# Loads of x gated by earlier batches, zero fills moved behind the softmax, the band copied in four pieces, and a new order, in a convolution and token-mixing kernel

## The chip, the cores and the metric

The kernel runs on one core of a Trainium2 chip. The metric is the device time of one execution in microseconds (us); lower is better. PE is the matrix engine (PEld its weight loads), DVE, ACT and POOL are the vector, scalar and general engines, SP is the engine that here only issues transfers. "A DMA" is a transfer that an engine issues and 16 DMA engines carry out.

## What is computed

```python
# x: (8, 4224, 192), weight: (8 heads, 7 taps)
w = softmax(weight)                       # over the 7 taps
x_pad = zeros of 6 rows in front of x
out[b, s, head, g] = sum_k w[head, k] * x_pad[b, s + k, head, g]     # 24 columns g a head
x = out
wq, wk = x @ w_q, x @ w_k                 # (8, 4224, 64)
W_tok = (1 / 8) * einsum('bsd,btd->bst', wq, wk)
mixed = einsum('bst,btd->bsd', W_tok, x)  # 4224 x 4224 weights a batch, never formed
result = relu(mixed) @ w_out              # (8, 4224, 192) float32
```

Since nothing nonlinear stands between the products, `mixed = wq @ (w_k.T @ (x.T @ x)) / 8`: a 192 x 192 Gram matrix a batch takes the place of the token weights.

## The kernel before, in words

**Stages of a batch.** A batch of 4224 rows is cut into 35 chunks of 122 rows. A chunk of x is loaded with the 6 rows before it, 128 rows in all, and turned from float32 to bfloat16 by the load itself (`XW`, which holds all eight batches; issued by POOL, L565). The causal convolution is a matmul with a banded 128 x 128 matrix a head (`BAND`): `conv`, L651, four operations of two heads each for a group of chunks (groups of 9 chunks in batch 0, of 18 and 17 in the others, L315). ACT or DVE copies the result to `Y` (L671). PE then transposes Y (`tr_lo` L691, `tr_hi` L726; copies by DVE, L698 and L733), forms wq from the transposes (`wq`, L751 and L755, five operations a batch, j = 0 to 4), and adds up the Gram matrix from Y itself (L787). A small product chain (L808 to L861) makes the 192-wide mixing matrix of the batch. Then, for each of five token blocks, `mix_lo` (L878) and `mix_hi` (L890) apply it to wq, ACT and DVE take the relu (L907, L908), `fin_hi` (L935) and `fin_lo` (L955) multiply by w_out, ACT or DVE copies to one of four output slots (L970), and SP stores the slot (L978). `mix_lo` and `fin_hi` use the array as two halves of 64 rows, all others as two halves of 64 columns. The helper `halves` (L391, L392) issues the two column halves of `conv`, of `fin_lo` and of some smaller products, `turn_halves` (L395, L396) those of the transposes, so that these lines stand for several stages and the tile names tell them apart.

**What sets the order.** Every operation is entered in a planner with its engine or engines, an estimated length in ns, the operations that it needs, and a due time. The due times of the program text (`vt=`) are not used: `add` (L381) takes them one by one from the list `TURNS`. The planner lays the operations one after another on five engine queues by its estimates; among the operations that are ready on an engine, it takes the one with the lowest due time, where PE adds `STAY` to an operation that would change its way of halving the array. The result is a fixed order on each engine. An engine waits (with semaphores) before an instruction for what the instruction needs; `after` only orders the planning. An engine never passes over an instruction that waits.

**Start.** DVE fills small tiles (L409 to L422), among them zeros in the tiles that need them only later (`zero_w`, `zero_yt`, `zero_q`, two `zero_k`, `zero_m`). SP loads `weight` (L402). POOL builds the identity `IDENT` (L426), from which DVE makes `step`, `other`, `own` (L435 to L457). Then the softmax: `mx` (L461, needs `weight`), `sub`, `mine`, ACT's exponentials `ex` (L482), `sm`, `rc`, `wn`, `taps` (L494, needs `own`). PE spreads the taps into two banks with eight matmul pairs (`fill`, L512), and ACT copies the one bank, DVE the other, into `BAND` (L527): two copies of 512 columns. All convolutions need both.

**Loads of x.** `gen_load` (L535) makes for each group one DMA of its whole chunks, and one each for the first chunk of a batch and for the last, short one: 34 in all. In batch 0 a DMA brings 7 to 9 chunks, in the others 17 or 16. They wait for no step of the computation: POOL issues them one behind the other from the start, and the planner takes it that a group lands at 5000 ns plus 260 ns for each chunk so far (`at`, L559). The three weight matrices are loaded by SP once group 1 of batch 0 has landed (L589).

**The loop.** Batch b's conv, transposes, wq, Gram and mixing matrix are entered together with the `mix` blocks of batch b - 1 (L988 to L1007). Y and wq are kept for two batches.

Of the kernel before, what the change touches and what calls it, by code (L numbers as in the profile page):

```python
# [13 lines left out]
    int(t) / 1000  # L14
    for t in """
# [50 lines left out]
""".split()  # L66
]

COL2, ROW2 = "128x64", "64x128"


class Op:


    n = 0

# [27 lines left out]
class Planner:  # L104

    LAT = {"PE": 240.0, "ACT": 145.0, "DVE": 140.0, "POOL": 150.0, "SP": 0.0}
    SWITCH = 145.0

    STAY = 0.865

    HOLD = 1

    def __init__(self, nbank, first_bank):
        self.ops = []
        self.order = []
# [162 lines left out]
def bass_lightweight_conv__then__hypermixer_token_mlp_kernel(  # L280
# [25 lines left out]
    t = 0  # L306
# [173 lines left out]
    def exps(e, op):  # L480
# [19 lines left out]
        220, wn, -7.5,  # L500
    )
    taps.needs.append(own)


    bands = []
    for q0, engine in ((0, "ACT"), (4, "DVE")):
# [552 lines left out]
```

## Time and profile before

| | |
|---|---|
| median of 3 executions | 177.7 us (177.54 to 178.31) |
| the profiled execution | 177.53 us, of it 175.7 us from the first to the last instruction (the span) |
| DVE busy | 118.0 us (67%) |
| ACT busy | 123.5 us (70%) |
| POOL busy | 30.3 us (17%), the last load issued at 52.5 us |
| loads of x | 13.61 MB written as bfloat16 |
| stores | 44 DMAs, 25.95 MB |
| batch 0: first conv, first Gram | 8.8 us, 13.1 us |
| first conv of batches 1 to 7 | 23.5, 34.4, 47.7, 67.9, 90.2, 105.7, 129.7 us |

How to read the profile: times are us from the first instruction. A row of the timeline has the start, the length, the engine, the line, the operation, what it writes and reads, and in brackets how long the engine stood idle before it and what ended that. "issue" as the end of an idle time means that the engine waited for nothing that the profile shows. A row of the windows has, for a stretch of time, the busy us of each engine with the count of its instructions, the granted clock, the DMA share (time of all queues' packets over that of 16 DMA engines, above 1 where packets of two queues overlap) and the GB/s. The DMA queue q0 carries the loads of x, q1 the other loads and the stores, q8 instructions. In the list of loads, "to landing" counts from the issue.

### The profile page before, as it was taken

The numbers are of one execution on the slowest core, as the hardware profiler recorded it, in microseconds if no ns is written. First come the engines' busy times: TensorE is split into PE (matmuls) and PEld (weight loads), VectorE is DVE, ScalarE is ACT, GpSimd is POOL, SyncE is SP. The second block draws the span as 40 slices with busy tenths as digits, with TensorE's granted clock in tenths as the row PEclk, the third lists the DMA queues.
The fourth block names the chain that finished last, engine by engine and source line by source line (L and its number), as shares of the span: only waits on it lengthen the run. The fifth ranks groups of instructions, "written<-read, shape, count | busy, mean of one in ns | idle before, by whom it ended". The sixth has DMA issues, their size and how long they took to land.

```text
span 175.7 us, 7099 instructions
## 1 busy us (share of the span) xinstructions
PE 157.1 (89%) x3226; PEld 121.7 (69%) x3226; DVE 118.0 (67%) x216; ACT 123.5 (70%) x206; POOL 30.3 (17%) x39
## 2 busy tenths in 40 slices
PE   0289799888999999899989979999999999999990
PEld 0179666776787787668778766878767777877550
DVE  6556587765766677586787738689688675765740
ACT  3243677597787948668648747888888896698980
POOL 7999452524230000000000000000000000000000
PEclk9999999999999999999999999999999999999995
DMA  3999999999999999999999999067283045987787
GB/s 30 162 189 186 205 191 193 191 196 277 193 279 194 286 309 268 343 250 243 304 264 282 237 194 348 24 244 297 103 343 127 4 175 216 356 347 309 265 303 262
DMA packets 48157, 40.36 MB, mean 230 GB/s; under 512 B 37632, under 2 KB 40960, under 8 KB 48128
## 3 DMA queue, kind: packets, MB, share of 16 engines
q0 software_dynamic: 36128, 13.61, 65.1%
q1 hardware_dynamic: 12000, 26.31, 40.9%
q8 instruction: 25, 0.41, 0.9%
q14 instruction: 4, 0.03, 0.1%
HBM read 27.56 MB, written 25.95 MB: 305 GB/s over the span
## 4 chain that ended last, share of the span: by engine, by line
PE 88%; issue 4%; DVE 3%; ACT 2%
PE ps L391 25%; PE ps L787 14%; PE ps L935 8%; PE ps L392 7%; PE ps L395 6%; PE ps L726 6%; PE ps L878 5%; PE ps L751 4%; PE ps L890 4%; PE ps L755 4%; PE ps L396 3%; ACT rt L907 1%; ACT out_sb L970 1%; DVE band L527 0%; DVE xw L416 0%
## 5 line engine op out<-in xcount | busy, mean ns | idle before, releaser
L970 ACT COPY out_sb<-ps 128x768 f32<-128x768 f32 (+1 forms) x46 | 34.7, 768 | 15.1 <-PE ps L392 11.3
L671 ACT CAST y<-ps 122x816 bf16<-122x816 f32 (+3 forms) x46 | 35.7, 791 | 13.2 <-PE ps L392 12.8
L907 ACT ACTIVATE rt<-ps 128x1024 bf16<-128x1024 f32 (+3 forms) x44 | 34.1, 800 | 6.4 <-PE ps L878 4.5
L787 PE MATMUL ps<-y 122*64 122x192 bf16 (+4 forms) x840 | 33.8, 222 | 2.2 <-issue 2.2
L970 DVE COPY out_sb<-ps 128x768 f32<-128x768 f32 (+1 forms) x26 | 21.6, 840 | 19.7 <-PE ps L392 18.5
L392 PE MATMUL ps<-wol,rt 128*64 128x192 bf16 x264 | 33.9, 255 | 1.0 <-issue 1.0
L787 PEld LDWEIGHTS ps<-y 122*64 122x64 bf16 (+1 forms) x840 | 31.1, 112 | 4.9 <-issue 2.8
L565 POOL DMA_DIRECT2D xw<-in_x_dram x34 | 29.9, 893 | 22.3 <-issue 21.5
L391 PE MATMUL ps<-wol,rt 128*64 128x192 bf16 x264 | 33.7, 255 | 0.0
L391 PE MATMUL ps<-xw,band 128*64 128x432 bf16 (+3 forms) x144 | 31.8, 335 | 1.5 <-DVE band L527 0.9
L392 PE MATMUL ps<-xw,band 128*64 128x432 bf16 (+3 forms) x144 | 32.1, 337 | 1.1 <-issue 1.1
L391 PEld LDWEIGHTS ps<-wol,rt 128*64 128x64 bf16 x264 | 24.1, 138 | 8.1 <-issue 2.0
L908 DVE TENSOR_SCALAR rt<-ps 128x512 bf16<-128x512 f32 (+3 forms) x36 | 23.6, 674 | 8.2 <-PE ps L878 7.6
L671 DVE CAST y<-ps 122x864 bf16<-122x864 f32 (+3 forms) x26 | 23.6, 912 | 8.0 <-PE ps L392 7.5
L698 DVE COPY ytl<-ps 128x976 bf16<-128x976 bf16 (+1 forms) x40 | 23.0, 591 | 3.9 <-PE ps L396 3.3
L392 PEld LDWEIGHTS ps<-wol,rt 128*64 128x64 bf16 x264 | 24.1, 138 | 1.2 <-issue 1.2
L396 PE MATMUL ps<-ident,y 122*64 122x122 bf16 x280 | 21.1, 219 | 0.0
L395 PE MATMUL ps<-ident,y 122*64 122x122 bf16 x280 | 21.0, 219 | 0.0
L935 PE MATMUL ps<-woh,rt 64*128 64x192 bf16 x264 | 20.4, 250 | 0.2 <-ACT rt L907 0.2
L395 PEld LDWEIGHTS ps<-ident,y 122*64 122x64 bf16 x280 | 18.1, 112 | 2.0 <-issue 0.5
L726 PE MATMUL ps<-ident,y 122*64 122x122 bf16 (+1 forms) x344 | 17.1, 220 | 1.3 <-DVE y L671 0.7
L396 PEld LDWEIGHTS ps<-ident,y 122*64 122x64 bf16 x280 | 17.7, 112 | 0.0
(95 smaller groups left out, 218.8 us busy)
## 6 DMA issues: line engine op xcount, KB each, us to landing
out_dram<-out_sb SPq DMA_DIRECT2D x28, 768.0 KB, 5.1
xw<-in_x_dram POOLq DMA_DIRECT2D x7, 816.0 KB, 33.2
xw<-in_x_dram POOLq DMA_DIRECT2D x7, 768.0 KB, 33.7
out_dram<-out_sb SPq DMA_DIRECT2D x8, 384.0 KB, 3.3
xw<-in_x_dram POOLq DMA_DIRECT2D x2, 432.0 KB, 8.3
out_dram<-out_sb SPq DMA_DIRECT2D x8, 96.0 KB, 4.3
xw<-in_x_dram POOLq DMA_DIRECT2D x1, 384.0 KB, 5.2
xw<-in_x_dram POOLq DMA_DIRECT2D x8, 45.8 KB, 25.0
```

The costliest lines, as they stand in the source:

```text
L391: e.matmul(out[0:64], lhsT[:, 0:64], rhs, **k)
L392: return e.matmul(out[64:128], lhsT[:, 64:128], rhs, **k)
L395: e.transpose(out[0:64], in_[:, 0:64], identity)
L396: return e.transpose(out[64:128], in_[:, 64:128], identity)
L565: lambda e, op, part=part: e.dma_start(*part),
L671: return e.copy(dst, src) if op.engine == "ACT" else e.tensor_copy(dst, src)
L726: last = e.transpose(ps[64 * i : 64 * i + HI, o : o + w], Y[0:w, yb, c, LO:D], IDENT[0:w, 0:w])
L787: mm = e.matmul(bank(GB)[p : p + 64, o : o + z - r], Y[0:w, yb, c, r : r + 64], Y[0:w, yb, c, r:z], start=st, stop=end, skip_group_check=True,
L907: return e.activation(dst, src(), AF.Relu)
L908: return e.tensor_scalar(dst, src(), 0.0, None, op0=ALU.max)
L935: last = e.matmul(bank(op.bank + a)[:, o : o + D], RT[64 * a : 64 * a + HI, slot, 2, i:n:nt], WOH[64 * a : 64 * a + HI, :], start=i == q, ...
L970: return e.copy(dst, src) if op.engine == "ACT" else e.tensor_copy(dst, src)
```

## The change

1. **Loads in four parts, paced.** From batch 1 on, the whole chunks of a group are loaded by two DMAs, the first with half of them rounded up: 9 and 8 chunks, 8 and 8. With the first and the last chunk that is six DMAs a batch and 48 in all. Each now needs a step of an earlier batch (a wait on POOL). For batch 1: the first chunk and first half of group 0 wait for group 2 of batch 0 to have landed, the second half for batch 0's last conv of group 2; group 1's first half waits for batch 0's last conv, the rest for its `wq` j = 0. For batch b from 2 on: first chunk and first half of group 0 wait for `wq` j = 0 of batch b - 2, the second half for j = 1; group 1's first half for j = 2, the rest for j = 3. The loads are entered in the planner beside the conv of their group. The planner now counts 4500 ns from issue to landing from batch 1 on, and fixed landing times in batch 0 (6000, 9900, 12300, 13900 ns).
2. **Zeros behind the softmax.** The six zero fills named above come after `taps` in DVE's order. The due time of `own` goes from -9.28 to -8.19, between `mine` (-8.21) and `sm` (-8.16); before, it stood right behind `other` (-9.29).
3. **Band in four pieces.** Four fills of two matmul pairs each (256 columns), four banks, four copies: ACT, DVE, ACT, DVE.
4. **Order.** All due times of the main part are new, `STAY` goes from 0.865 to 0.954561. The estimates of `ident` (1250 to 700), of the fills (260 to 200) and of the band copies (550 to 340) change with it.

```diff
@@ -11,58 +11,90 @@
 
 
 TURNS = [
-    int(t) / 1000
+    int(t) / 1e6
     for t in """
...
 """.split()
 ]
 
@@ -108,9 +140,9 @@
     LAT = {"PE": 240.0, "ACT": 145.0, "DVE": 140.0, "POOL": 150.0, "SP": 0.0}
     SWITCH = 145.0
 
-    STAY = 0.865
-
-    HOLD = 1
+    STAY = 0.954561
+
+    HOLD = 1.000000
 
     def __init__(self, nbank, first_bank):
         self.ops = []
@@ -426,7 +458,7 @@
         lambda e, op: e.affine_select(
             IDENT[:, :], IDENT[:, :], [[-1, 128]], ALU.is_equal, 0.0, base=0, channel_multiplier=1
         ),
-        1250,
+        700,
         needs=[one],
         vt=-9,
     )
@@ -455,7 +487,7 @@
     own = add(
         "DVE",
         lambda e, op: e.tensor_reduce(OWN[:, :], IDENT[:, :].rearrange("p (k i) -> p i k", i=16), AX.X, ALU.add),
-        200, needs=[ident], vt=-8.92)
+        200, needs=[ident], vt=-7.83)
 
 
     mx = add("DVE", lambda e, op: e.tensor_reduce(WMX[:, :], WT_F[:, :, :], AX.X, ALU.max), 150, needs=[load_w], vt=-8)
@@ -501,38 +533,43 @@
     )
     taps.needs.append(own)
 
+    for zero in (zero_w, zero_yt, zero_q, *zero_k, *(zero_m if isinstance(zero_m, list) else [zero_m])):
+        zero.after.append(taps)
+
 
     bands = []
-    for q0, engine in ((0, "ACT"), (4, "DVE")):
+    for q0, engine in ((0, "ACT"), (2, "DVE"), (4, "ACT"), (6, "DVE")):
 
         def spread(e, op, q0=q0):
             last = None
-            for q in range(q0, q0 + 4):
+            for q in range(q0, q0 + 2):
                 last = halves(
                     e,
                     bank(op.bank)[:, (q - q0) * 128 : (q - q0 + 1) * 128],
                     STEPT[0:112, 112 - 16 * q : 240 - 16 * q],
                     TAPS[0:112, :, :].rearrange("p i h -> p (i h)"),
                     start=q == q0,
-                    stop=q == q0 + 3,
+                    stop=q == q0 + 1,
                     skip_group_check=True,
                 )
             return last
 
-        fill = add("PE", spread, 260, needs=[taps, stept], banks=1, vt=-7 + 0.1 * q0)
+        fill = add("PE", spread, 200, needs=[taps, stept], banks=1, vt=-7 + 0.1 * q0)
 
         def band(e, op, q0=q0, fill=fill):
-            dst = BAND[:, :, 16 * q0 : 16 * q0 + 64]
-            src = bank(fill.bank).rearrange("p (j h) -> p h j", h=H)
+            dst = BAND[:, :, 16 * q0 : 16 * q0 + 32]
+            src = bank(fill.bank)[:, 0 : 32 * H].rearrange("p (j h) -> p h j", h=H)
             return e.copy(dst, src) if op.engine == "ACT" else e.tensor_copy(dst, src)
 
-        bands.append(add(engine, band, 550, drains=fill, vt=-6.9))
+        bands.append(add(engine, band, 340, drains=fill, vt=-6.9))
 
 
     load = {}
-    at = [5000.0]
-
-    def gen_load(b, gi):
+
+    LANDS = [6000.0, 9900.0, 12300.0, 13900.0]
+
+    def gen_load(b, gi, gates=()):
+
         sem = semaphore(f"s_x{b}_{gi}")
         cs = groups_of(b)[gi]
         parts = []
@@ -540,13 +577,17 @@
         full = [c for c in cs if 0 < c < NCC - 1]
         if cs[0] == 0:
             parts.append((XW[KC - 1 : 128, b, 0, :], bass.AP(x_t, base, [[D, CW], [1, D]])))
-        n = len(full)
-        parts.append(
-            (
-                XW[:, b, full[0] : full[0] + n, :],
-                bass.AP(x_t, base + (CW * full[0] - KC + 1) * D, [[D, 128], [CW * D, n], [1, D]]),
+        cut = (len(full) + 1) // 2 if b else len(full)
+        for some in (full[:cut], full[cut:]):
+            if not some:
+                continue
+            parts.append(
+                (
+                    XW[:, b, some[0] : some[0] + len(some), :],
+                    bass.AP(x_t, base + (CW * some[0] - KC + 1) * D, [[D, 128], [CW * D, len(some)], [1, D]]),
+                )
             )
-        )
+        lead = 1 + (cs[0] == 0)
         if cs[-1] == NCC - 1:
             rows = S - (CW * (NCC - 1) - KC + 1)
             parts.append(
@@ -556,7 +597,6 @@
                 )
             )
 
-        at[0] += len(cs) * 260.0
         load[b, gi] = []
         for k, part in enumerate(parts):
             first = (b, gi) == (0, 0) and part[0].shape[1] > 1 and len(part[0].shape) == 3
@@ -564,13 +604,13 @@
                 "POOL",
                 lambda e, op, part=part: e.dma_start(*part),
                 900,
-                needs=[zero_x] if cs[-1] == NCC - 1 else [],
+                needs=[*([zero_x] if cs[-1] == NCC - 1 else []), *(gates[0 if k < lead else 1] if gates else [])],
                 after=[] if first else [ident],
                 dma=(f"x{b}_{gi}", sem, 16),
                 vt=-10 if first else -4 + b + gi * 0.1 + 0.02 * k,
             )
-            op.tail = 1500.0
-            op.lands = at[0]
+            op.tail = 1500.0 if b == 0 else 4500.0
+            op.lands = LANDS[gi] if b == 0 else 0.0
             load[b, gi].append(op)
 
     for gi in range(len(groups_of(0))):
@@ -615,14 +655,11 @@
         cast(WOH[:, :], WHI[:, OS], load_o),
     ]
 
-    for b in range(1, B):
-        for gi in range(len(groups_of(b))):
-            gen_load(b, gi)
-
 
     y_done, y_read = {}, {}
     yt_done, yt_read, yth_read, wq_read, rt_read, m_read = {}, {}, {}, {}, {}, {}
     g_read, gsb_read = None, None
+    conv_op, wq_op = {}, {}
     store_of = {}
     n_rt = n_out = 0
     S_OUT = [semaphore(f"s_o{i}") for i in range(NOUT)]
@@ -670,6 +707,7 @@
                 dst = dst.rearrange("p c (t g) -> p t c g", t=2)
                 return e.copy(dst, src) if op.engine == "ACT" else e.tensor_copy(dst, src)
 
+            conv_op[b, gi] = mm
             ev = add(both, evac, evac_ns(2 * n * GRP), needs=ev_needs, drains=mm, vt=vt, kind="y")
             for c in cs:
                 y_done.setdefault((b, c), []).append(ev)
@@ -759,6 +797,7 @@
 
         mq = add("PE", wq, mm_ns(n, 2), needs=[*{id(r): r for c in cs for r in yt_done[b, c]}.values(), turned, *casts_q],
             after=wfree, banks=1, vt=vt, kind="wq")
+        wq_op[b, j] = mq
         yth_read[b, j] = [mq]
         for c in cs:
             for g in range(0, NCC, 8):
@@ -989,6 +1028,10 @@
         nxt = []
         if b < B:
             for gi in range(len(groups_of(b))):
+                if b == 1:
+                    gen_load(b, gi, ([load[0, 2][-1]], [conv_op[0, 2]]) if gi == 0 else ([conv_op[0, 3]], [wq_op[0, 0]]))
+                elif b:
+                    gen_load(b, gi, ([wq_op[b - 2, 2 * gi]], [wq_op[b - 2, 2 * gi + 1]]))
                 gen_conv(b, gi)
             for c in range(0, NCC, 8):
                 gen_transpose(b, list(range(c, min(c + 8, NCC))))
```

132 rows, old and new, of the table TURNS are left out of this document.

## The prediction

> **What bounds the kernel now.** I read the page first, then PE's idle time by stretch, then what ended it, then the DMA queues in the same stretches.
>
> ```profile
> span 175.7 us, 7099 instructions
> ...
> PE 157.1 (89%) x3226; PEld 121.7 (69%) x3226; DVE 118.0 (67%) x216; ACT 123.5 (70%) x206; POOL 30.3 (17%) x39
> ```
>
> PE is the bound; the others have a third of the span free. So the question is where PE's 18.6 idle us lie. The windows start at the first convolution and break where the first three batches' loads are in, and where the last load is in:
>
> ```profile
> 8.76:33.40 24.64, 22.07 (x461) 18.38 (x463) 16.61 (x31) 14.49 (x32) 16.18 (x19) 1.00 1.57 193
> 33.40:104.50 71.10, 67.56 (x1432) 53.44 (x1432) 48.50 (x81) 50.51 (x82) 6.55 (x7) 1.00 1.37 257
> 104.50:165.00 60.50, 60.32 (x1245) 45.28 (x1239) 44.71 (x77) 50.54 (x83) 0.00 (x0) 1.00 0.58 221
> ```
>
> PE idles 2.57 us in the first stretch, 3.54 in the second, 0.18 in the third. The DMA share falls from 1.57 and 1.37 to 0.58 exactly where the idle time ends. What ended the idle time, from the waits of PE:
>
> ```profile
> PE ps L787 <- issue: 2.2, 2, 1.3
> PE ps L392 <- issue: 2.1, 2, 1.1
> PE ps L391 <- DVE band L527: 0.9, 1, 0.9
> PE ps L726 <- DVE y L671: 0.7, 1, 0.7
> PE ps L391 <- issue: 0.6, 1, 0.6
> PE ps L726 <- issue: 0.5, 1, 0.5
> ```
>
> Six stops of 0.5 to 1.3 us, 5.4 us together, ended by nothing that another engine did. With the 0.7 us for y they make up the 6.1 us of the first two stretches: all six lie there, 1.9 us in the first and 3.5 us in the second. I take them for PE running out of instructions. The DMA queues up to 104.5 us, and around the first stop:
>
> ```profile
> q0 software_dynamic: 35945, 13.54, 109.0%
> q1 hardware_dynamic: 4752, 10.09, 28.1%
> q8 instruction: 14, 0.23, 0.8%
> ```
>
> ```profile
> 19.03 0.17 PE ps L787 x5
> 19.20 1.28 issue
> 20.48 0.54 PE ps L787 x8
> ```
>
> ```profile
> q0 software_dynamic: 443, 0.17, 97.9%
> q1 hardware_dynamic: 222, 0.11, 40.2%
> q8 instruction: 1, 0.02, 4.2%
> ```
>
> The last fence is the window 17.9 to 19.3 us: one instruction packet of 0.02 MB moves just ahead of the stop, while loads hold the DMA engines 98% of the time. Up to 104.5 us 14 such packets share the engines with a load queue that is never empty, and six stops follow. Behind it no stop of this kind is left. So a fetch that queues behind loads comes late.
>
> [...]
>
> **Part 1, paced loads.** What it removes is backlog. Now the loads of all batches stand in q0 at once; with the gates at most about one batch does. How long a fetch can be held up then depends on how long a part takes. Two consecutive parts of batch 0, of 432 KB each (9 chunks, the new size):
>
> ```profile
> L565 POOL DMA_DIRECT2D xw<-in_x_dram x2: 991/992/992, 3.2 to 4.2; - x2
> ...
> DMA to landing us min/median/max: 7.6/8.3/8.9
> ```
>
> They landed at 3.2 + 7.6 = 10.8 and 4.2 + 8.9 = 13.1 us, so a part takes 2.3 us alone, and all of q0 (13.54 MB, 31 such parts) some 71 us; beside stores it took until 104.5. So with the gates loads are in flight about half to two thirds of the time, but in short runs: a fetch waits for one or two parts, not for an endless queue. Bounds of the gain: 0 (any load in flight delays a fetch as much as a full queue) and 5.4 us (no stop left). I keep the 1.9 us of the first stretch, since batches 0 to 2 are gated so early that q0 stays full to about 33 us, and a tenth of the 3.5 us, 0.35, because PE stopped only in six of 14 fetches, so that a shorter delay mostly disappears in the stock that PE still holds. Gain 3.15 us.
>
> What it adds: 14 DMAs. A 9-chunk issue costs POOL 0.99 us; POOL has nothing else to do (17% busy), so they cost nothing unless the load itself is late. The gates are waits on POOL, and behind a waiting load stand only later loads. Who waits for them is the conv of that group, and behind it everything on PE, because PE's order is fixed. How close is that? The five `wq` of batch 1, of which j = 0 to 3 will gate batch 3, then j = 1 alone, then batch 3's conv, as they stand now:
>
> ```profile
> L751 PE MATMUL ps<-ytl,wql x9: 219/379/379, 40.3 to 45.7; 128*64 128x512 bf16 x8, 128*64 128x128 bf16 x1
> ```
>
> ```profile
> L751 PE MATMUL ps<-ytl,wql x2: 379/379/379, 42.8 to 42.8; 128*64 128x512 bf16 x2
> ```
>
> ```profile
> L391 PE MATMUL ps<-xw,band x16: 333/343/370, 47.7 to 57.6; 128*64 128x432 bf16 x8, 128*64 128x408 bf16 x8
> ```
>
> The first load of x shows the time from issue to landing with an empty queue:
>
> ```profile
> L565 POOL DMA_DIRECT2D xw<-in_x_dram x1: 1010/1010/1010, 1.3 to 1.3; - x1
> ...
> DMA to landing us min/median/max: 5.2/5.2/5.2
> ```
>
> 5.2 us. With batch 3 gated from 40.3 us on, its first part lands by about 46.1 (the small DMA of chunk 0 is issued ahead of it, some 0.6 us), the second, gated at 42.8, by 48.0: 0.3 us behind the 47.7 at which the conv starts now. So the margin is small in the old order. The new order was laid out with the gates in it and 4.5 us of flight, so I charge 0.4 us for late loads in all, between 0 and the rival below.
>
> **Part 2, zeros and own.** DVE's row of work up to the taps, and the weights' load (issued by SP at 0.8 us, 2.9 us to landing):
>
> ```profile
> 3.02 0.11 DVE L417 MEMSET wqh<- 128x64 uint32 x1
> ...
> 3.42 0.12 DVE L435 COPY step<-ident 128x128 bf16<-128x128 bf16 x1
> ...
> 3.65 0.37 DVE L457 TENSOR_REDUCE own<-ident 128x16 f32<-128x128 bf16 x1
> 3.94 0.26 DVE L453 TENSOR_SCALAR other<-other 128x8 f32<-128x8 f32 x1
> 4.28 0.11 DVE L411 MEMSET yth<- 64x64 uint32 x1
> ...
> 4.70 0.15 DVE L461 TENSOR_REDUCE wmx<-wt_f 128x8 f32<-128x56 f32 x1
> ...
> 5.71 0.29 DVE L487 TENSOR_REDUCE wsm<-wex 128x16 f32<-128x128 f32 x1 [0.36 <-ACT wex L482]
> ...
> 7.93 0.69 DVE L527 CAST band<-ps 128x512 bf16<-128x512 f32 x1 [1.16 <-PE ps L392]
> ```
>
> ```profile
> wt_f<-in_weight_dram SPq DMA_DIRECT2D x1, 28.0 KB, 2.9
> ```
>
> Before `wmx` the zeros take 3.02 to 3.42 and 4.28 to 4.70, 0.82 us, and `own` 3.65 to 3.94, 0.29. Without these 1.11 us `wmx` could start at 3.6, but the weights land at 3.7; say 3.85 with the wake-up: 0.85 us earlier. `own` moves into the 0.36 us in which DVE waits for the exponentials, which covers its 0.37. The zeros, 0.82 us, move into the 1.16 us in which DVE waits for the fill; should that cover go, they would cost at most 0.82. Gain at the taps: 0.85 us.
>
> **Part 3, the band.** The copies now:
>
> ```profile
> 7.50 0.58 ACT L527 CAST band<-ps 128x512 bf16<-128x512 f32 x1 [1.82 <-PE ps L392]
> ```
>
> ```profile
> 8.76 0.36 PE L391 MATMUL ps<-xw,band 128*64 128x216 bf16 x1 [0.88 <-DVE band L527]
> ```
>
> DVE starts 0.43 us behind ACT, the time of half the fill, so a quarter takes 0.215. With quarters ACT can begin at 7.29, DVE at 7.50, ACT again at 7.72, DVE at 7.93. No row has a copy of 256 columns; it lies between half of 0.69 (0.35) and 0.69, and I take 0.4, near the half. The last copy then ends at 8.33 instead of 8.62: 0.25 to 0.29 us, zero at the upper bound. With part 2 the first conv starts some 1.1 us earlier, at 7.65. The first part of x landed at 1.3 + 5.2 = 6.5 us, so it is there.
>
> Not all of that reaches the end, for two reasons. Group 1 lands at 10.8, and its conv starts at 11.5 now. And PE is slow early on:
>
> ```profile
> 12.01 0.17 PE ps L391
> ...
> 15.92 0.09 PE ps L391
> ```
>
> Two steps of the same conv, first at 0.17 us a matmul, then at 0.09, although the granted clock of the page reads full. If the change of pace stays at about 15 us, what is won before it is worth half, 0.55 us; if it moves along, 1.1. I take 0.7.
>
> **Part 4, the order.** Nothing in the trace prices it. PE's busy time per matmul was 47.9, 47.2 and 48.4 ns in the three windows; that spread of 0.6 ns each way over 3226 matmuls is about 2 us, my bound to either side for an order that is better or worse packed. I take 0.
>
> **Sum.** The profiled execution took 177.53 us, 1.8 of it outside the span, and lies 0.2 below the median of 177.7. 177.53 - 3.15 - 0.7 + 0.4 = 174.1 us.
>
> **Rivals.**
>
> *The stops stay.* The load queue is in flight nearly as long as before, and each fetch that meets it is late all the same. For it: q0 needs 71 us alone, and with stores beside it took 101, so that about as many fetches meet a load. Against: the delays lie so near PE's stock that only six of 14 stopped it. Time: 177.53 - 0.7 + 0.4 = 177.2. [...]
>
> *Loads become the wait.* A gated part that shares the DMA engines with stores is slower by 101 / 71, so 3.3 us instead of 2.3, and the second part of a group lands 1 us late; PE stands still behind the conv. If that 1 us stops PE in half of the twelve groups of batches 2 to 7, it is 6.0 us in place of the 0.4: 179.7. It decides from about 0.3 us a group, where it eats the 3.85 us won. For it: 40.3 and 47.7 above, and the order is planned without stores in the DMA engines' way. Against: Y must be free before a conv, which usually keeps it well behind these `wq`.
>
> *Everything works and the order is better.* All stops go (another 2.2 us), no load is late: 171.5.
>
> **How the numbers follow.** Forecast 174.1, chance 0.55; stops stay, 177.2, 0.18; loads late, 179.7, 0.17; everything, 171.5, 0.10. A measurement of this kernel tells about 0.5% (0.9 us) from no change, so "same" is 176.8 to 178.6. Faster: the forecast, the best case, and a part (0.05) of the stops' case, which lies at its edge: 0.70. Same: the rest of it, 0.13. Slower: 0.17, the late loads. The range runs from the best case to the milder half of the late loads, 171.5 to 178.8; some 0.05 is left out below and 0.1 above. The forecast's own range is 172.3 to 175.9 (the order's 2 us, cut a little).
>
> **What would show it.** First conv at 7.5 to 7.9 us. Stops ended by "issue" on PE of 2 us or less in all, most of them before 35 us. Load issues on POOL out to about 130 us and loads landing some 5 to 8 us after issue. PE idle before conv on a load of x: below 0.5 us. I am wrong if the "issue" stops keep their 5 us, or if PE waits for "DMA xw" by microseconds.

## The result and the profile after

The changed kernel takes 207.9 us (median of four executions, 204.0 to 210.6) beside 177.85 us for the kernel before: 1.15 times the time (95% interval 1.142 to 1.161). Of this kernel and some below, part of the executions took some us longer than the rest; the ratios leave these out, but the profiled execution is such a long one here (210.6 beside 204.0 and 205.7) and in the runs with small stores, group 0 first, gates a batch earlier and two groups, so that the rows below hold those us too.

The page of the changed kernel, span and engines, then the chain that ended last; the last row is the chain of the kernel before:

```profile
span 208.3 us, 7102 instructions
...
PE 165.1 (79%) x3226; PEld 128.2 (62%) x3226; DVE 122.4 (59%) x217; ACT 121.2 (58%) x207; POOL 38.7 (19%) x53
...
PE 55%; DMA 31%; DVE 4%; POOL 3%; ACT 2%; issue 2%
```

```profile
PE 88%; issue 4%; DVE 3%; ACT 2%
```

Nearly a third of the chain is now transfers; its row had none before. PE is busy 8 us longer with the same 3226 matmuls, and it idles 43 us instead of 18.6. PE's waits (L423 and L424 of the changed kernel are `halves`, L427 and L428 `turn_halves`):

```profile
PE ps L423 <- DMA xw<-in_x_dram: 27.7, 7, 8.8
PE ps L427 <- DVE step L467: 3.3, 1, 3.3
PE ps L423 <- DVE taps L526: 2.6, 1, 2.6
PE ps L826 <- issue: 0.8, 1, 0.8
```

Seven times PE stands before a convolution whose x has not landed, 27.7 us in all and up to 8.8 at a time. The stops that "issue" ends went from 5.4 to 0.8 us. The windows run from the first convolution to 33.8 us, on to the last landing of a load at 161.6, and from there to 198; the first column behind the length is PE's busy time, the third from the end the granted clock:

```profile
7.90:33.80 25.90, 24.33 (x457) 20.42 (x457) 16.56 (x29) 14.98 (x35) 9.52 (x13) 1.00 1.35 159
33.80:161.60 127.80, 99.29 (x2000) 76.91 (x2000) 70.23 (x120) 70.63 (x112) 23.70 (x30) 0.90 0.97 188
161.60:198.00 36.40, 36.08 (x694) 27.29 (x692) 26.85 (x41) 29.08 (x50) 0.00 (x0) 0.98 0.61 233
```

The loss lies in the second stretch, as long as gated loads are in flight: 28.5 us idle, at a granted clock of 0.90 (1.00 before). Where no load is left, PE is as full as before (36.08 of 36.40 us).

**One of the waits.** The chain and POOL's timeline around the longest wait, before batch 6's first convolution:

```profile
117.32 0.22 PE ps L793 x2
117.54 0.27 PE ps L764 x10
...
118.01 13.96 DMA xw<-in_x_dram
...
132.01 0.57 PE ps L423
```

```profile
109.78 1.54 POOL L605 DMA_DIRECT2D xw<-in_x_dram  x2 [14.99 <-PE ps L793]
117.02 1.87 POOL L605 DMA_DIRECT2D xw<-in_x_dram  x2 [5.70 <-PE ps L424]
121.36 1.42 POOL L605 DMA_DIRECT2D xw<-in_x_dram  x2 [2.47 <-PE ps L793]
```

POOL issues the first part of group 0 at 109.8 us, then idles until the next `wq` steps. The row at 117.0 holds two loads, and the first of them is already group 1's first half: the new order places it ahead of group 0's second half. That one goes out at 118.0 and lands 13.96 us later; PE stands from 123.2 to 132.0. On POOL itself the place cost little, since the gate of the second half, `wq` j = 1, ends on PE at 117.5 only: the new order runs j = 2 ahead of it. But 384 KB more then stand ahead of it in the load queue. The planner counted 4.5 us for the flight. All parts, by their size, with the median in us; those issued after 33 us took 5 to 14 us:

```profile
xw<-in_x_dram POOLq DMA_DIRECT2D x22, 384.0 KB, 8.3
xw<-in_x_dram POOLq DMA_DIRECT2D x9, 432.0 KB, 8.9
```

**Why the flight is long.** The DMA queues of the changed kernel in two stretches of 2 us, 90 to 92 with a store in flight, and 99 to 101 without:

```profile
q1 hardware_dynamic: 220, 0.67, 85.3%
q0 software_dynamic: 170, 0.06, 25.4%
```

```profile
q0 software_dynamic: 927, 0.35, 147.8%
q1 hardware_dynamic: 2, 0.00, 0.5%
```

Beside a store the load queue moves 0.06 MB where alone it moves 0.35: a sixth. In the long wait itself, from 126 to 128 and to 130 us, it moves 0.09 and 0.08, a quarter. The packets of the two queues are of like number (170 and 220; 237 and 185, 208 and 212 in the long wait), but a load's packet writes 384 bytes and a store's 3 KB. At like counts the bytes went with the size of the packets: 0.06 MB of loads beside 0.67 MB of stores from 90 to 92 us, 0.09 and 0.08 beside 0.57 and 0.61 in the long wait.

**The clock.** Windows of the changed kernel from that wait on; the column ahead of the last two is the granted clock:

```profile
123.00:132.00 9.00, 0.20 (x2) 0.00 (x0) 1.26 (x2) 0.80 (x1) 0.00 (x0) 0.64 1.29 292
132.00:134.00 2.00, 1.99 (x23) 1.44 (x25) 0.00 (x0) 0.88 (x1) 0.00 (x0) 0.50 0.90 107
134.00:136.00 2.00, 2.00 (x28) 1.38 (x26) 1.06 (x1) 0.77 (x1) 0.00 (x0) 0.55 0.00 0
136.00:138.00 2.00, 2.00 (x49) 1.63 (x47) 1.03 (x3) 1.73 (x3) 0.00 (x0) 1.00 0.00 0
```

After the wait PE runs at half its clock for some 4 us, 23 and 28 matmuls in 2 us instead of 49. So this wait is paid twice. At the three longest waits (5.5, 6.3 and 8.8 us), by windows of 1 us, the clock fell 2.3 to 4.7 us after PE stopped, to 0.50, and came back 3.6 to 5.2 us after PE began again.

**The head.** The taps of the kernel before, then DVE and PE of the changed kernel:

```profile
6.47 0.29 DVE L494 TENSOR_TENSOR taps<-own,wtap 128x128 bf16<-128x128 f32 x1
```

```profile
3.71 0.49 DVE L493 TENSOR_REDUCE wmx<-wt_f 128x8 f32<-128x56 f32 x1
...
5.85 0.29 DVE L526 TENSOR_TENSOR taps<-own,wtap 128x128 bf16<-128x128 f32 x1
...
7.07 0.69 DVE L562 CAST band<-ps 128x256 bf16<-128x256 f32 x2
```

```profile
7.90 0.36 PE L423 MATMUL ps<-xw,band 128*64 128x216 bf16 x1 [0.64 <-DVE band L562]
```

Taps 0.62 us earlier, the last band copy done at 7.76 instead of 8.62, the first convolution at 7.90 instead of 8.76.

### The profile page after: what moved, and what is told of

The parts are those of the page before. It is cut to its first block, busy times and chain, and to the rows that moved or that the text cites. A ratio compares the mean times of both kernels' runs of the same rounds, so it can differ in the third digit from the quotient of the medians.

```text
span 208.3 us, 7102 instructions
## 1 busy us (share of the span) xinstructions
PE 165.1 (79%) x3226; PEld 128.2 (62%) x3226; DVE 122.4 (59%) x217; ACT 121.2 (58%) x207; POOL 38.7 (19%) x53
## 4 chain that ended last, share of the span: by engine, by line
PE 55%; DMA 31%; DVE 4%; POOL 3%; ACT 2%; issue 2%
DMA xw<-in_x_dram 31%; PE ps L423 20%; PE ps L826 9%; PE ps L974 5%; PE ps L427 4%; PE ps L764 4%; PE ps L917 3%; POOL xw L605 3%; PE ps L424 3%; PE ps L789 3%; PE ps L793 2%; PE ps L929 2%; PE ps L428 2%; DVE rt L947 1%; ACT out_sb L1009 1%
## 5 line engine op out<-in xcount | busy, mean ns | idle before, releaser
L708 ACT CAST y<-ps 122x816 bf16<-122x816 f32 (+3 forms) x50 | 37.8, 781 | 53.7 <-PE ps L424 50.8
L605 POOL DMA_DIRECT2D xw<-in_x_dram x48 | 38.3, 803 | 111.7 <-PE ps L793 48.8
L423 PE MATMUL ps<-xw,band 128*64 128x408 bf16 (+3 forms) x144 | 36.5, 385 | 28.3 <-DMA xw<-in_x_dram 27.7
L1009 DVE COPY out_sb<-ps 128x768 f32<-128x768 f32 (+1 forms) x31 | 28.3, 918 | 27.4 <-PE ps L424 25.5
L708 DVE CAST y<-ps 122x864 bf16<-122x864 f32 (+3 forms) x22 | 20.6, 936 | 32.4 <-PE ps L424 32.0
L423 PEld LDWEIGHTS ps<-xw,band 128*64 128x64 bf16 x144 | 16.6, 132 | 34.5 <-DMA xw<-in_x_dram 29.0
L826 PE MATMUL ps<-y 122*64 122x192 bf16 (+4 forms) x840 | 35.9, 231 | 1.6 <-issue 0.8
L424 PE MATMUL ps<-xw,band 128*64 128x408 bf16 (+3 forms) x144 | 36.5, 385 | 0.0
L1009 ACT COPY out_sb<-ps 128x768 f32<-128x768 f32 (+1 forms) x41 | 29.5, 730 | 11.7 <-PE ps L424 10.8
L423 PE MATMUL ps<-wol,rt 128*64 128x192 bf16 x264 | 33.0, 256 | 0.0
L424 PE MATMUL ps<-wol,rt 128*64 128x192 bf16 x264 | 32.9, 256 | 0.0
L423 PEld LDWEIGHTS ps<-wol,rt 128*64 128x64 bf16 x264 | 24.0, 139 | 7.2 <-issue 1.8
L424 PEld LDWEIGHTS ps<-wol,rt 128*64 128x64 bf16 x264 | 24.0, 139 | 0.0
L427 PE MATMUL ps<-ident,y 122*64 122x122 bf16 x280 | 22.3, 224 | 0.7 <-ACT y L708 0.7
L428 PE MATMUL ps<-ident,y 122*64 122x122 bf16 x280 | 22.4, 225 | 0.0
L427 PEld LDWEIGHTS ps<-ident,y 122*64 122x64 bf16 x280 | 19.2, 116 | 2.9 <-ACT y L708 1.1
L428 PEld LDWEIGHTS ps<-ident,y 122*64 122x64 bf16 x280 | 18.9, 116 | 0.2
```

What stands on the lines that cost most here:

```text
L423: e.matmul(out[0:64], lhsT[:, 0:64], rhs, **k)
L424: return e.matmul(out[64:128], lhsT[:, 64:128], rhs, **k)
L427: e.transpose(out[0:64], in_[:, 0:64], identity)
L428: return e.transpose(out[64:128], in_[:, 64:128], identity)
L605: lambda e, op, part=part: e.dma_start(*part),
L708: return e.copy(dst, src) if op.engine == "ACT" else e.tensor_copy(dst, src)
```

## The experiments

Theory A: the gates open too late for the flight that a load has beside stores, and everything else is small. Rivals: the new order is slow by itself (B), or 48 smaller loads are slower than 34 (C). Beside that stands the theory of the prediction, that a deep load queue starves PE of instructions. Where not said otherwise, an edit is made after planning, so that every engine keeps its order.

**No gates.**

```diff
...
+    for ops in load.values():
+        for op in ops:
+            op.needs = [x for x in op.needs if x not in op.gates]
```

> The changed kernel with its order, its head and its 48 loads as they are, but no load waits for a step of an earlier batch. Theory A (the gates open too late: a load flies 8 to 14 us beside stores where the plan counts 4.5, and PE stands before the convolution): the 27.7 us of PE's waits on loads go, the clock stays full, 173 to 179 us, with stops ended by issue back at 3 to 6 us. Rival B (the new order is itself slow on the chip) and rival C (48 smaller loads are slower than 34): 195 us or more.

178.4 us, 1.0054 times the kernel before (1.003 to 1.0079), so half a per cent above it. No wait of PE on a load is left. The span and engines, and PE's stops:

```profile
PE 155.4 (88%) x3226; PEld 122.6 (70%) x3226; DVE 122.0 (69%) x217; ACT 120.6 (69%) x207; POOL 38.7 (22%) x53
```

```profile
PE ps L827 <- issue: 2.3, 3, 1.4
PE ps L427 <- issue: 1.7, 1, 1.7
PE ps L423 <- issue: 0.7, 1, 0.7
PE ps L424 <- issue: 0.6, 1, 0.6
PE ps L765 <- issue: 0.2, 1, 0.2
```

The gates alone make the loss. Between the two profiled executions, 210.56 and 178.08, it adds up: 27.7 us of waits, 9.7 of longer busy time of PE (165.1 and 155.4), less 4.7 of "issue" stops (0.8 and 5.5): 32.7 of 32.5. Of the 9.7 us, 7.8 are the lower clock, if in windows of 1 us PE's busy time is taken times the missing share of the granted clock; the rest is not traced. B and C fall as causes of the loss.

**The planner told 11 us.** The changed kernel with its gates, planned anew.

```diff
...
-            op.tail = 1500.0 if b == 0 else 4500.0
+            op.tail = 1500.0 if b == 0 else 11000.0
```

> The changed kernel with its gates, planned with 11 us in place of 4.5 us from the issue of a load to its landing, so that the planner lays other work before the convolutions. Theory A: PE waits on loads fall from 27.7 us to under 8 us, 183 to 193 us. If the estimate is not what is wrong: 203 to 210 us as the changed kernel.

193.0 us, 1.085 (1.079 to 1.091). PE's wait on loads:

```profile
PE ps L423 <- DMA xw<-in_x_dram: 5.5, 4, 3.5
```

With a flight nearer to the measured one, the waits mostly go, so the estimate made most of them. Yet the time is 15 us above that without gates. Of the 14.3 us between the two spans (190.0 and 175.7), 10.3 are PE's busy time, 165.7 us for the same 3226 matmuls at a granted clock of 0.99, so this is not the clock. What in the new plan makes it longer is not shown; its due times were laid out for 4.5 us. This estimate does not make the gates pay.

**Small stores.** The changed kernel with its gates; each store writes an eighth of its columns.

```diff
...
+                    few = (qz - qa) * D // 8
...
```

> The changed kernel with its gates, and each store writes an eighth of its columns, so that most of the output stays unwritten. If loads are late because stores share the DMA engines with them: flights of loads fall from a median of 8 to 9 us to 5 to 6 us, PE's waits on loads from 27.7 to under 8 us, 180 to 186 us. If the gates open too late even for a quiet queue: waits stay above 18 us, 198 us or more.

179.5 us (176.6 to 180.4). Flights and waits:

```profile
xw<-in_x_dram POOLq DMA_DIRECT2D x22, 384.0 KB, 6.0
xw<-in_x_dram POOLq DMA_DIRECT2D x9, 432.0 KB, 7.1
```

```profile
PE ps L423 <- DMA xw<-in_x_dram: 8.2, 5, 1.7
```

Flights, waits and time lie at the edge of what was expected for this theory, mostly just outside it (5 to 6 us, under 8 us, 180 to 186 us), and far from the other (above 18 us of waits, 198 us or more). Of the 27.7 us, 19.5 come from the stores beside the loads; since the small stores also have small packets, the run does not tell bytes from packet size. The rest, 8.2 us, the gates make even so, in waits of at most 1.7 us, and PE is then busy 157.5 us: these short waits cost little clock, 1.6 us by the same windows, all of it around 37 to 41 us.

**Group 0 first on POOL.** The changed kernel with its gates; in batches 2, 6 and 7 group 1's first half goes behind group 0's second half.

```diff
...
+    for b in range(1, B):
+        half0, half1 = load[b, 0][-1], load[b, 1][0]
+        if order.index(half1) < order.index(half0):
+            order.remove(half1)
+            order.insert(order.index(half0) + 1, half1)
```

> The changed kernel with its gates; on POOL, group 1's first half no longer stands ahead of group 0's second half in batches 2, 6 and 7. If this place in POOL's queue makes the longest waits (8.8 us in batch 6): waits on loads fall from 27.7 to 16 to 20 us, 195 to 199 us. If flight under stores and the gates alone make them: 25 us or more, 203 to 208 us.

203.8 us (197.1 to 204.5).

```profile
PE ps L423 <- DMA xw<-in_x_dram: 20.4, 8, 3.9
```

The place in POOL's queue made 7 of the 27.7 us and the longest waits; without it the longest is 3.9 us. The waits just miss what was expected for this (16 to 20 us). The median time, 203.8, does not tell the two theories apart: it lies where the other one put it (203 to 208 us), the shortest execution in 195 to 199. And PE is still busy 164.7 us, as in the changed kernel: behind waits of 3.4 and 3.9 us the granted clock still falls to 0.50, 6.9 us of loss in all by windows of 1 us.

**Gates a batch earlier.** The changed kernel's order, loads of batch b from 3 on behind `wq` of batch b - 3, those of batches 1 and 2 free.

```diff
...
+            op.needs = [x for x in op.needs if x not in op.gates]
+            if b >= 3:
+                op.needs.append(wq_op[b - 3, 2 * gi + (k >= lead)])
```

> The changed kernel with its order, but loads of batch b from 3 on wait for the wq steps of batch b - 3 in place of b - 2, and batches 1 and 2 wait for nothing. Theory A: no wait of PE on a load over 1 us, 172 to 177 us. The theory that a deep load queue starves PE of instructions, as the prediction had it: stops ended by issue at most 2 us, 2 to 4 us below the kernel without gates; if depth does not matter, both are equal within 1 us. Rival B: 195 us or more.

180.3 us, 1.0092 (1.0046 to 1.0138). No wait on loads, but:

```profile
PE ps L827 <- issue: 3.3, 4, 1.2
PE ps L424 <- issue: 2.5, 2, 2.2
PE ps L427 <- issue: 1.8, 1, 1.8
PE ps L794 <- issue: 0.4, 1, 0.4
```

8.0 us of stops with a shallow queue, beside 5.5 with the deep one of the kernel without gates. That speaks against the theory of depth, which asked for at most 2 us. It does not show that a shallow queue is worse: the ten executions took 177.7 to 181.2 us, and were all the 3.5 us between them stops of the profiled one, 4.5 would be left.

**The kernel before, gated.** Its own order and 34 loads; batch b from 3 on behind `wq` j = 0 and j = 2 of batch b - 3.

```diff
...
+            gate = wq_op[b - 3, 2 * gi]
...
+            for op in load[b, gi]:
+                op.needs.append(gate)
```

> The kernel before, its order and its 34 loads, with the loads of batch b from 3 on made to wait for wq j = 0 (group 0) and j = 2 (group 1) of batch b - 3. Nothing else is changed. If a deep load queue starves PE of instructions: stops ended by issue fall from 5.4 to 2 us, 174 to 175.5 us. If only the presence of a load matters: stops stay at 4 to 5.5 us, 177 to 178 us. If even this gate is too late: PE waits on loads, 179 us or more.

178.8 us, 1.0063 (1.0029 to 1.0098). None of the three outcomes expected came about. The "issue" stops fall to 2.6 us, all of them before 41 us; until 38 us the load queue is still as full as without gates (0.37 to 0.39 MB in 2 us from 20 us on), since only batch 3's loads have been held by then. But output copies now wait for their slot; the last row is the kernel before:

```profile
DVE out_sb L972 <- DMA out_dram<-out_sb: 5.7, 4, 2.4
ACT out_sb L972 <- DMA out_dram<-out_sb: 2.8, 1, 2.8
```

```profile
ACT out_sb L970 <- DMA out_dram<-out_sb: 2.4, 1, 2.4
```

Stores of 768 KB land in 6.8 us instead of 5.1, and PE stands 3.0 us on output copies that are late. What the loads gave back in stops, the stores took.

**No loads behind batch 0.** The kernel before (first) and the changed one without gates (second), with the loads of batches 1 to 7 left out; their convolutions read batch 0's x.

```diff
...
-                        XW[:, b, c0 : c0 + n, GRP * h : GRP * h + GRP],
+                        XW[:, 0, c0 : c0 + n, GRP * h : GRP * h + GRP],
...
+    planner.order = [op for op in planner.order if op not in later_loads]
```

> The kernel before, its order, with the loads of batches 1 to 7 left out: their convolutions read batch 0's x again, so that seven eighths of the output are not the reference's. If loads in flight make PE's stops that end by issue: they shrink from 5.4 to below 1 us, 172 to 174 us, and this is what no arrangement of the loads can beat in this order. If the stops have another cause: 177 us or more.

> The changed kernel, its order and its head, with the loads of batches 1 to 7 and their gates left out in the same way (convolutions of batches 1 to 7 read batch 0's x). Beside the kernel before without these loads it prices the new order and the new head alone: 0.7 us below it if the order packs PE as well as before, 1 us or more above it if the new order is worse packed.

169.7 us (0.955, 0.950 to 0.960) and 170.6 us (0.959, 0.955 to 0.963).

```profile
PE 154.5 (92%) x3226; PEld 121.1 (72%) x3226; DVE 117.7 (70%) x216; ACT 123.7 (74%) x206; POOL 5.6 (3%) x11
```

```profile
PE 153.6 (91%) x3226; PEld 121.8 (72%) x3226; DVE 121.7 (72%) x217; ACT 120.7 (72%) x207; POOL 5.6 (3%) x11
```

In neither does PE stop on "issue" once. So loads in flight cost the kernel before 8.3 us: the 5.4 us of stops, 2.6 us of PE's busy time, and a little elsewhere. That is the most that another arrangement of the loads could win in this order, and more than was expected (172 to 174 us). And with the loads out of the picture the new order and head are 0.95 us slower, though the head starts 0.86 us earlier. With the loads in, without gates, the two kernels differ by about as much (178.4 and 177.6), so that 48 loads in place of 34 cost nothing by themselves.

**The head alone.** The kernel before with the zeros behind the taps and the band in quarters.

```diff
...
+    order[at_band:at_band] = zeros + f4 + b4
...
```

> The kernel before, its order and its loads, with the new head alone: six zero fills behind the taps, and the band filled and copied in four quarters. Prediction's step: first convolution 0.9 to 1.1 us earlier, of which 0.4 to 1.1 us reach the end, 176.5 to 177.2 us beside 177.6. Rival: x and y hold PE back at the start as before, no change.

`f4` and `b4` are four fills and four copies. 176.9 us, 0.9939 (0.9912 to 0.9965): 1.1 us faster than the kernel before, with the convolution's start where the changed kernel has it:

```profile
7.91 0.36 PE L391 MATMUL ps<-xw,band 128*64 128x216 bf16 x1 [0.64 <-DVE band L532]
```

This is the one part of the change that pays, by 0.6%, and of the versions that compute the whole result the only one that is shown to beat both kernels.

**Two groups, or one, in the load queue.** The kernel of the last run; a group's loads wait for the landing of the group two (one) places earlier, and for no step of PE.

```diff
...
+    for k in range(2, len(groups)):
+        for op in groups[k]:
+            op.needs.append(max(groups[k - 2], key=order.index))
```

> The kernel before with the new head (as in the run of the head alone), and each group's loads wait on POOL until the group two places earlier has landed, so that at most two groups stand in the load queue; nothing waits for a step of PE. The theory that the depth of the load queue starves PE: stops ended by issue fall from about 5 to below 2.5 us and the time from 176.9 to 174 to 175.5 us. Rival, that the mere presence of a load does it: stops stay at 4 to 6 us, 176.5 to 177.5 us. If two groups in flight are too few to keep up: PE waits on loads, above 178 us.

> The same with one group in the load queue at a time. Depth theory: stops ended by issue below 1.5 us. Presence theory: they go down only with the pauses between groups, 3 to 5 us. Either way loads come later; if PE waits on them, 178 to 190 us.

With two groups 179.1 us, but six executions spread from 174.8 to 180.4, so its time is inconclusive. PE's waits:

```profile
PE ps L391 <- DMA xw<-in_x_dram: 1.8, 2, 1.6
PE ps L392 <- issue: 1.7, 2, 1.3
PE ps L792 <- issue: 0.9, 1, 0.9
PE ps L731 <- issue: 0.8, 1, 0.8
PE ps L940 <- issue: 0.5, 1, 0.5
```

3.9 us of stops beside 5.0 for the head alone: in this execution little was gained from a queue of a fraction of the depth. The shortest execution took what the theory of depth expected (174 to 175.5 us), and it is one of six and has no profile. With one group 225.9 us, 1.27 (1.263 to 1.275): 38.6 us of waits on loads, and even so 3.4 us of "issue" stops, where depth asked for less than 1.5. A shallow queue does not end them.

## Why the prediction was wrong

It forecast 174.1 us, and 207.9 was measured. The step that failed is the charge for late loads: "The new order was laid out with the gates in it and 4.5 us of flight, so I charge 0.4 us for late loads in all". Measured were 27.7 us of waits, and 9.7 us more of PE's busy time behind them, 7.8 of it by the lower clock. The prediction had the mechanism among its rivals, with a chance of 0.17, but priced it at 6.0 us, and its 179.7 was far too low as well. Three things were missed in the size.

- **The flight.** It was taken from a load into an empty queue (5.2 us), and beside stores slowed by 101 / 71, an average over a stretch in which stores were in flight only part of the time. In the windows beside a store the load queue moved 0.06 to 0.09 MB in 2 us, a sixth to a quarter of the 0.35 that it moved alone, and parts took 5 to 14 us. The profile of before shows the like: from 60 to 62 us, with a store in flight, q0 moved 0.11 MB in 293 packets beside 0.50 MB of q1 in 291.
- **The margin.** It was read from the old order, at one batch. But a planner that counts 4.5 us may place the convolution just behind that; its estimate should have been set against the measured flight at once, and against 5.2 us it was short even for an empty queue. Planned with 11 us, the waits fall to 5.5.
- **The clock.** That PE would be granted half its clock behind late loads (0.50 after the waits of 5.5, 6.3 and 8.8 us) was not in the sum. The early matmuls at half pace (0.17 us, later 0.09) were seen, and taken for a matter of the start only; the granted clock reads 1.00 there, so that they have the same cause is not shown.

The other steps:

- **"issue" stops.** That loads in flight cause them is shown: they are gone without loads. That the depth of the queue does it, on which the 3.15 us rested, did not hold: stops of 8.0, 3.9 and 3.4 us remained with shallow queues, beside 5.5 and 5.0 with deep ones. In the changed kernel they fell to 0.8 us, as forecast, but while PE stood still elsewhere; that sign came true by luck.
- **What the stops are.** The prediction took them for PE running out of instructions, and the traces bear that out more closely than it could say. If all records of PE are counted, those of its sequencer among them, the six stops of the kernel before come ahead of record 450, 962, 1218, 2498, 3266 and 3778, always a multiple of 256 apart; all 47 stops of these eleven traces stand at such places. Nearly all end 2.2 to 2.5 us (one 2.9) after the start of an instruction packet in q8, which holds 16 KB. Up to 104.5 us these packets start when PE has 44 to 121 records left to the next such place; with the later loads left out, the same 14 packets start with 172 to 266 left, and no stop follows. The packets themselves take no longer than without loads (0.89 to 0.98 us, without 0.88 to 1.66), so a fetch is late because it begins late. What sets how late, and why the gated kernel before has no stop past 41 us while the order of the changed one with gates a batch earlier has most of its 8.0 us there, stays open.
- **Head.** Predicted 1.1 us at the first convolution, and 0.7 at the end; measured 0.86 and 1.1 (the interval runs from 0.6 to 1.6). `own` did not move behind `mine`: DVE took it while it waited for the weights, at 3.27 us, and the weights, which landed at 3.7, set the start of `wmx` as predicted. The 0.15 us of wake-up in the prediction's 3.85 was the author's estimate, which no run shows; `wmx` began at 3.71. But `wmx` then took 0.49 us instead of 0.15, so that the taps came 0.62 us earlier and not 0.85; the four pieces brought the remaining 0.24, about as predicted.
- **Order.** Taken as 0 within 2 us; the two runs without loads put it at about 1.8 to 2.0 us worse (0.95 plus the 0.86 to 1.1 of the head).
- **POOL.** The extra issues cost nothing by themselves, as said (48 loads without gates). But "behind a waiting load stand only later loads" was no comfort: group 0's second half was one of them.

## What to carry to other kernels

A wait put ahead of a transfer must be earlier than its use by the longest flight that the trace shows under the traffic of that stage (here 14.0 us), not by the flight into an empty queue (5.2 us); where a planner has a number for it, set that against the trace before anything else. Loads that ran far ahead cost 8.3 of 178 us here; loads that came late cost 27.7 us of waits, and 7.8 us of clock behind them. Ask of a paced queue what stands ahead of the urgent transfer, too. And where an engine stops with nothing to wait for, count its instructions up to each stop: here all distances were multiples of 256, and that pointed at the fetch.

## What the runs showed of the hardware that was not expected

- A load queue with 384-byte packets kept a sixth to a quarter of its rate beside stores with packets of 3 KB (0.06 to 0.09 and 0.35 MB in 2 us), at like counts of packets.
- After waits of 5.5, 6.3 and 8.8 us PE was granted half its clock for some 4 to 5 us, after one of 2.2 us for 3.0 us (37.3 to 40.2 us); with group 0 first this came behind waits of 3.4 and 3.9 us as well, while a wait of 3.5 us in the run planned with 11 us cost no clock at all (1.00 from 40 to 50 us).
- Loads in flight cost PE 8.3 of 178 us without a single wait on a load: 5.4 us of stops, at places in PE's instructions that lie multiples of 256 apart, and 2.6 us in busy time.
